# Head, tile slots and last tile of a fused linear-attention and feed-forward kernel moved

## The chip, the cores and the metric

The kernel runs on one core of one Trainium2 chip. The metric is the device time of one execution in microseconds; before the change the median of 12 executions is 298.38 us (297.88 to 298.96).

## The reference

Eight batches of 8 heads, 576 positions and 64 channels per head go through linear attention without softmax, an RMS norm per head, and a feed-forward block with a layer norm in front and a residual around it (model width 512, hidden width 2048):

```python
kv = np.einsum('bhsd,bhse->bhde', k, v)
out = np.einsum('bhsd,bhde->bhse', q, kv)
rms = np.sqrt(np.mean(out * out, axis=-1, keepdims=True) + 1e-06)
attn = out / rms * g_norm                 # then (b, h, s, d) -> x of shape (b, s, 512)

mu, var = mean and variance of x over the 512 channels
xn = (x - mu) / np.sqrt(var + 1e-06) * g_ln
y = x + np.maximum(xn @ w_ch1, 0.0) @ w_ch2
```

## The kernel before

**Tiles.** A batch has 576 positions: four main tiles of 128, and 64 left over. Two batches share one remainder tile, so every odd batch (1, 3, 5, 7) adds one. The order of the feed-forward work on TensorE is fixed: batch 0 to 7, then a block "rem" of the four remainder tiles. Each block is a first stage `mm1` (L391: x times w1, ScalarE evacuates with a ReLU, L404) and a second stage `mm2` (L438: times w2, 16 matmuls per tile, L417; VectorE adds the residual in `finish`, L422, and SyncE writes the tile out in two halves, L435 and L436).

**Slots.** Everything else (attention, norms, turns, loads) is hung between these matmuls. `at(slot, fn)` (L457) enters a function into an agenda, and `tick` (L460), called before every group of 16 matmuls or so (a PSUM bank of `mm1`, four matmuls of `mm2`), runs what stands under the slot's whole number, in order of the fraction. A block has 32 slots: 16 of the first stage, then 16 of the second; batch b starts at slot 32b. A slot sets only the place in each engine's instruction stream; each engine works its own stream in order, and waits on semaphores for the others. GpSimd's and SyncE's streams hold mainly DMA issues and so run far from the slot's time.

**A tile.** `o` (L254) multiplies q, turned, by the block-diagonal kv of two heads; `sq` squares it on ScalarE (L265), `red` sums on VectorE (L286), `root` takes the root on ScalarE (L296), then on VectorE `inv` (L303), `y` (L291), `x` (L310, with the sum for the mean) and `xc` (L320, mean removed and scaled by g_ln). `var` (L328, ScalarE) gives the variance, used only in `finish` as `rstd`. `turn` (L331) brings xc into the layout that `mm1` takes, in four 128x128 transposes on TensorE and a ScalarE copy (L336, L338), or with one DMA transpose from SyncE (L340). `plan_tile` (L359) puts o, sq and red at slot s, y, x and xc at s + 2, var at s + 6, and the turn at a slot given to it.

**q and kv.** `kv_of(b)` (L228) makes kv in 40 matmuls and two ScalarE copies. From batch 2 on, q is turned by `turn_q_dma` (L199): a VectorE copy into q_p (L201), then one DMA transpose from SyncE into qt (L203). `load_batch` (L96) issues six loads of k, v and q from GpSimd, behind a one-element copy from qt of the batch before (L98), so that they start when that turn has landed.

**PSUM.** Eight banks in four pools: `ps_m` ("misc", 1), `ps_out` ("ops", 2, products of tiles), `ps1` ("p1", 3, first stage), `ps2` ("p2", 2, second stage).

**The head.** Batch 0 has no earlier matmuls to hide behind. `fill` (L193) runs dummy matmuls while k and v load. `kv_first` (L207) makes kv of batch 0, and kv_g, the same scaled by g_norm. Tiles 0 and 1 are then done in halves of four heads: `half_o` (L485) turns the q of both tiles on TensorE with 64x64 transposes (`turn_groups`, L177), copies the turns to SBUF (ScalarE for the first half, VectorE for the second, L490), and multiplies by kv (L497). `half_sq` (L503) and `half_red` (L507) follow; `o_g` and `x_g` (L267, L274) take x from the product with kv_g, which saves the y step. The xc of tile 0 is made and turned in two column halves (L529 to L534). The q of tiles 2, 3 and of the remainder is turned later by `turn_first` (L188), in slots.

Of the kernel before, what the change touches and what calls it, by code (L numbers as in the profile page):

```python
# [14 lines left out]
def kernel(  # L15
# [11 lines left out]
    nc = tc.nc  # L27
# [160 lines left out]
    def turn_first(i, pool, tag):  # L188
        tp = pool.tile([128, HP, 128], bf16, tag=tag, name="tp")
        n = turn_groups(tp, i, 0, H)  # L190
        nc.scalar.copy(qts[0][:, i, :, :n], tp[:, :, :n])

    def fill(n):  # L193
        for _ in range(n):
            p1 = ps2.tile([128, 512], f32, tag="p2", name="p1")
            nc.tensor.matmul(p1, lhsT=fill_sb[:, :128], rhs=fill_sb, start=True, stop=True)  # L196
            del p1
# [145 lines left out]
    def main_tile(b, j, pool=None, tag="ops"):  # L343
        q_t, kvp = qts[b], held[b]
        if b not in blks:
            blks[b] = new_block("main", 3)
        return Tile([(slice(0, 128), lambda hp: q_t[:, j, hp, :], kvp)], blks[b], j, pool, tag)
# [90 lines left out]
    def mm2(b, split_last=False):  # L438
        for ts in range(4):
            if split_last and ts == 3:  # L440
                for c0 in (0, Dm // 2):
                    p2 = ps2.tile([128, Dm], f32, tag="p2", name="p2")
                    mm2_part(b, ts, p2, 0, nDe, c0, c0 + Dm // 2)
                    finish(b, ts, p2, c0, c0 + Dm // 2, both=True)
                    del p2
            else:
                p2 = ps2.tile([128, Dm], f32, tag="p2", name="p2")
                mm2_part(b, ts, p2, 0, nDe)
                finish(b, ts, p2)
                del p2  # L450
        del blks[b], m1s[b]
# [22 lines left out]
    fill(24)  # L474
# [3 lines left out]
    t = [main_tile(0, i) for i in range(4)]  # L478
# [6 lines left out]
    def half_o(half):  # L485
        hp0 = half * HP // 2
        tp = ps2.tile([128, 2, HP // 2, 128], bf16, tag="p2", name="tp")
        for i in range(2):
            turn_groups(tp[:, i], i, 2 * hp0, 2 * hp0 + H // 2)
            copies[half][i](qts[0][:, i, hp0:hp0 + HP // 2], tp[:, i])  # L490
        res = []
        for i in range(2):
            pool, tag = banks[half][i]
            o = pool.tile([128, H // 2, D], f32, tag=tag, name="o_half")
            flat = o.rearrange("p h e -> p (h e)")
            for k2 in range(HP // 2):
                nc.tensor.matmul(flat[:, k2 * 128:(k2 + 1) * 128], lhsT=qts[0][:, i, hp0 + k2, :],  # L497
                                 rhs=kv_pack[0][:, hp0 + k2, :], start=True, stop=True)
            res.append(o)
        return res  # L500

    def half_sq(i, half, o):
        nc.scalar.activation(sqs[i][:, half * H // 2:(half + 1) * H // 2], o, func=AF.Square)  # L503
# [4 lines left out]

    oa = half_o(0)
    half_sq(0, 0, oa[0])  # L510
    half_sq(1, 0, oa[1])
    ob = half_o(1)
    half_sq(0, 1, ob[0])
    half_sq(1, 1, ob[1])
    for half in range(2):
        half_red(0, half)
    half_red(1, 0)
    half_red(1, 1)
    del oa, ob, sqs
    t[0].o_g(ps1, "p1")  # L520
    t[1].o_g(ps1, "p1")
    fill(5)
    t[0].x_g()
    t[1].root()
    x_blk, st, xT = t[0].blk
    for i in range(2):
        cs = slice(i * Dm // 2, (i + 1) * Dm // 2)
        xc = work.tile([128, Dm // 2], bf16, tag="xch", bufs=2, name="xc")
        nc.vector.scalar_tensor_tensor(xc, in0=x_blk[:, 0, cs], scalar=st[:, 1, 0:1],  # L529
                                       in1=g_ln_sb[:, cs], op0=ALU.add, op1=ALU.mult)  # L530
        tp = ps_out.tile([128, 2, 128], bf16, tag="ops", name="tp")
        for kk in range(2):
            nc.tensor.transpose(tp[:, kk, :], xc[:, kk * 128:(kk + 1) * 128], identity)
        nc.scalar.copy(xT[:, 2 * i:2 * i + 2, :128], tp)  # L534
        del xc, tp
    t[1].x_g()
    t[1].xc()
# [24 lines left out]
    at(0, lambda: turn_first(2, ps_m, "misc"))  # L562
    at(2, lambda: t[1].turn(True))
    at(2.1, o2)
    at(2.2, x2)
    at(4, lambda: turn_first(3, ps_m, "misc"))
    at(5, lambda: t[3].o())
    at(5.5, x3)
# [3 lines left out]
    at(11, lambda: t[3].turn(True))  # L572
# [20 lines left out]
    for j, s, tn in ((0, 24, 29), (1, 27, 34), (2, 31, 38), (3, 35, 42)):  # L593
        plan_tile(s, lambda j=j: main_tile(1, j), tn, True)
# [9 lines left out]
    at(47, lambda: load_batch(3, qts[2][:1, J, HP - 1, 127:]))  # L604
    at(57, lambda: kv_of(3))
    at(57.5, lambda: turn_q_dma(3))
    for b in range(3, B):
        s = 32 * b
        if b > 3:
            at(s - 60, lambda b=b: load_batch(b, qts[b - 1][:1, J, HP - 1, 127:]))  # L610
            at(s - 39, lambda b=b: kv_of(b))
            at(s - 38, lambda b=b: turn_q_dma(b))
        for j in range(J):
            o = s - 28 + (0, 5, 10, 15)[j]
            plan_tile(o, lambda b=b, j=j: main_tile(b, j), o + 6, False)
        if b % 2:
            plan_tile(s - 11, lambda b=b: rem_tile(b), s - 5, False)
        at(s + 14, lambda b=b: rstd_of(b))
# [58 lines left out]
```

## Time and profile before

| | |
|---|---|
| Median of 12 executions | 298.38 us (297.88 to 298.96) |
| The execution that was profiled | 297.88 us |
| Its span, first to last instruction | 296.1 us |
| TensorE busy | 282.8 us (96%) |
| ScalarE, VectorE busy | 157.2 us, 149.7 us |
| Granted TensorE clock, mean | 0.998 |
| First matmul with w1 | 16.98 us from the span's start |
| End of the last matmul | 292.08 us |

A row of a timeline gives start, duration, engine, line, operation, what is written from what, shapes, and how often; in brackets stands the idle time ahead of it and what ended it. A wait row gives who waited for whom: total, times, longest. "L401 PE" is TensorE at line 401 of the kernel. Matmuls overlap, so a row's duration is longer than its share of the engine: a 128x512 matmul lasts 379 ns and the next starts 216 ns after it. Durations of copies and of VectorE operations overlap their successors by some 60 to 80 ns.

### The profile page before, as it was taken

The page shows a single profiled execution, that of the slowest core. Times are in us where ns is not written, and L with a number is a line of the kernel's source. Part 1 is how long each engine was busy: PE and PEld are TensorE (multiplying, and loading weights), DVE is VectorE, ACT ScalarE, POOL GpSimd, SP SyncE. Part 2 cuts the span into 40 slices and gives each one's busy share as a digit, 9 for nine tenths or more (in the row PEclk, how much of TensorE's full clock was granted, in tenths as well). Part 3 has the DMA queues.
Part 4 walks back from the last instruction along what each step waited for, and adds up shares of the span by engine and source line. Part 5 has one row for each costly group of instructions (what it writes and reads, how often), then busy time and mean ns, then how long its engine had stood idle before and what let it go on. Part 6 is the DMA issues. An engine that isn't in the chain of part 4 may idle for free.

```text
span 296.1 us, 5729 instructions
## 1 busy us (share of the span) xinstructions
PE 282.8 (96%) x2280; PEld 159.3 (54%) x2305; DVE 149.7 (51%) x332; ACT 157.2 (53%) x341; POOL 40.7 (14%) x68
## 2 busy tenths in 40 slices
PE   8879999999999999999999999999999899999994
PEld 3469854996579644445444544444444344444443
DVE  5657018836995794468246953692369500220022
ACT  3457754886559742774187517931793266016500
POOL 8433500032023000500050005000000000000000
PEclk9999999999999999999999999999999999999999
DMA  7999999469579926995799249967312330131033
GB/s 214 203 206 203 201 202 198 95 99 185 119 144 175 138 54 130 166 194 81 149 169 164 55 93 158 202 110 136 78 35 44 69 84 0 38 74 32 0 73 71
DMA packets 63130, 35.84 MB, mean 121 GB/s; under 512 B 30716, under 2 KB 58108, under 8 KB 63104
## 3 DMA queue, kind: packets, MB, share of 16 engines
q0 software_dynamic: 28016, 17.76, 42.3%
q1 hardware_dynamic: 34656, 16.99, 28.3%
q10 hardware_dynamic: 432, 0.72, 0.7%
q8 instruction: 18, 0.29, 0.4%
q14 instruction: 8, 0.07, 0.1%
HBM read 36.71 MB, written 9.44 MB: 156 GB/s over the span
## 4 chain that ended last, share of the span: by engine, by line
PE 74%; DVE 12%; ACT 4%; DMA 4%; issue 3%; SPq 1%; DVEq 0%
PE p L401 38%; PE p L417 28%; DMA qt<-q_p 3%; DVE x_blk L310 2%; PE p L196 2%; DVE y L291 2%; PE o_ps L259 2%; DVE o_sb L422 2%; ACT m L404 2%; DVE xc L320 1%; PE kv_ps L234 1%; DVE ss L286 1%; DMA xT_blk<-xc 1%; PE tp L183 1%; PE tp L336 1%
## 5 line engine op out<-in xcount | busy, mean ns | idle before, releaser
L401 PE MATMUL p<-xT_blk,w_sb 128*128 128x128 bf16 (+2 forms) x1015 | 131.2, 285 | 1.5 <-ACT xT_blk L338 0.7
L417 PE MATMUL p<-w_sb,m 128*128 128x512 bf16 (+1 forms) x576 | 128.6, 373 | 2.8 <-DVE o_sb L422 1.4
L404 ACT ACTIVATE m<-p 128x512 bf16<-128x512 f32 x144 | 85.7, 597 | 65.9 <-PE p L401 64.7
L401 PEld LDWEIGHTS <-w_sb 128*128 128x128 bf16 x1024 | 78.5, 98 | 46.5 <-issue 2.0
L417 PEld LDWEIGHTS <-m 128*128 128x128 bf16 x592 | 56.2, 98 | 62.0 <-issue 2.3
L422 DVE SCALAR_TENSOR_TENSOR o_sb<-p,rstd,x_blk 128x512 f32<-128x512 f32 (+1 forms) x37 | 27.0, 732 | 43.1 <-PE p L417 40.4
L286 DVE TENSOR_REDUCE ss<-sq 128x8 f32<-128x512 f32 x34 | 23.2, 683 | 26.5 <-ACT sq L265 26.5
L328 ACT ACTIVATE dev<-x_blk,st_blk 128x512 f32<-128x512 f32 x36 | 25.8, 716 | 7.2 <-DVE st_blk L314 7.2
L265 ACT ACTIVATE sq<-o_ps 128x512 f32<-128x512 f32 x34 | 20.2, 595 | 15.5 <-PE o_ps L259 15.2
L320 DVE SCALAR_TENSOR_TENSOR xc<-x_blk,st_blk,g_ln_sb 128x512 bf16<-128x512 f32 x35 | 26.3, 751 | 1.2
L291 DVE TENSOR_TENSOR y<-o_ps,inv 128x512 f32<-128x512 f32 x34 | 23.5, 692 | 2.7
L310 DVE SCALAR_TENSOR_TENSOR x_blk<-y,g_norm_sb 128x512 f32<-128x512 f32 x34 | 23.5, 692 | 1.2
L410 DVE RECIPROCAL rstd<-rstd 128x4 f32<-128x4 f32 x9 | 1.6, 174 | 39.8 <-ACT rstd L409 39.8
L296 ACT ACTIVATE rms<-ss,eps_sb 128x8 f32<-128x8 f32 x36 | 10.8, 301 | 14.0 <-DVE ss L286 13.6
L303 DVE RECIPROCAL inv<-rms 128x8 f32<-128x8 f32 x36 | 7.2, 199 | 21.4 <-ACT rms L296 21.3
L98 POOL COPY gate<-qt 1x1 bf16<-1x1 bf16 x5 | 0.9, 177 | 123.3 <-DMA qt<-q_p 123.3
L259 PEld LDWEIGHTS <-qt 128*128 128x128 bf16 (+1 forms) x152 | 9.9, 100 | 8.3 <-issue 1.7
L259 PE MATMUL o_ps<-kv_pack,qt 128*128 128x128 bf16 (+1 forms) x152 | 13.3, 220 | 0.7 <-DMA qt<-q_p 0.7
L196 PE MATMUL p<-fill_sb 128*128 128x512 bf16 x29 | 8.3, 450 | 1.2 <-DVE eps_sb L137 1.2
L338 ACT COPY xT_blk<-tp 128x512 bf16<-128x512 bf16 x11 | 6.4, 582 | 3.4 <-PE tp L336 3.4
L328 ACT ACTIVATION_READ_ACCUMULATOR dev<-x_blk,st_blk 128x1 f32 x36 | 6.9, 192 | 0.0
L234 PEld LDWEIGHTS <-k_in 128*64 128x64 bf16 x280 | 5.4, 112 | 2.6 <-issue 2.5
(78 smaller groups left out, 116.0 us busy)
## 6 DMA issues: line engine op xcount, KB each, us to landing
out_dram<-o_sb SPq DMA_DIRECT2D x70, 128.0 KB, 2.4
w_sb<-in_moe_w_ch_dram POOLq DMA_DIRECT2D x8, 512.0 KB, 14.0
k_in<-in_k_dram POOLq DMA_DIRECT2D x7, 320.0 KB, 5.5
v_in<-in_v_dram POOLq DMA_DIRECT2D x7, 320.0 KB, 8.1
q_in<-in_q_dram POOLq DMA_DIRECT2D x7, 320.0 KB, 10.3
q_in<-in_q_dram POOLq DMA_DIRECT2D x8, 256.0 KB, 11.0
k_in<-in_k_dram POOLq DMA_DIRECT2D x7, 256.0 KB, 6.5
v_in<-in_v_dram POOLq DMA_DIRECT2D x7, 256.0 KB, 8.8
```

What stands on the lines that cost most here:

```text
L196: nc.tensor.matmul(p1, lhsT=fill_sb[:, :128], rhs=fill_sb, start=True, stop=True)
L259: nc.tensor.matmul(flat[rows, hp * 128:(hp + 1) * 128], lhsT=lhsT_of(hp), rhs=kvp[:, hp, :], start=True, stop=True)
L265: nc.scalar.activation(self.sq_t, self.o_ps, func=AF.Square)
L286: nc.vector.tensor_reduce(self.ss, self.sq_t, axis=AX.X, op=ALU.add)
L291: nc.vector.tensor_mul(self.y_t, self.o_ps, self.inv().to_broadcast([128, H, D]))
L310: nc.vector.scalar_tensor_tensor(x_blk[:, ts].rearrange("p (h d) -> p h d", h=H), in0=self.y_t, scalar=1.0, in1=g_norm_sb.to_broadcast([12 ...
L320: nc.vector.scalar_tensor_tensor(self.xc_t, in0=x_blk[:, self.ts], scalar=st[:, 1, self.ts:self.ts + 1], in1=g_ln_sb, op0=ALU.add, op1=ALU ...
L328: nc.scalar.activation(dev, x_blk[:, ts], func=AF.Square, bias=st[:, 1, ts:ts + 1], accum_out=st[:, 2, ts:ts + 1])
L401: nc.tensor.matmul(p1[:, i, :], lhsT=w1_sb[:, kk, de * 128:(de + 1) * 128], rhs=blk[2][:, kk, sl], start=(kk == 0), stop=(kk == nK - 1))
L404: nc.scalar.activation(m1[:, de0:de0 + per, sl], p1, func=AF.Relu)
L417: nc.tensor.matmul(p2[:, c0:c1], lhsT=m1s[b][:, de, ts * 128:(ts + 1) * 128], rhs=w2_sb[:, de, c0:c1], start=(de == 0), stop=(de == nDe - 1))
L422: nc.vector.scalar_tensor_tensor(o_sb[:, c0:c1], in0=p2[:, c0:c1], scalar=rstds[b][:, ts:ts + 1], in1=blks[b][0][:, ts, c0:c1], op0=ALU.mu ...
```

## The change

- **Fills.** 18 in place of 24 at the start; two more after the first turns, in the pool of tile products; 8 in place of 5 ahead of tile 0's xc.
- **Tiles 0 and 1.** The turns of both tiles stand ahead of their copies, each in a PSUM tile of its own. The products come one by one, each with its square, between the turns of the second half. The root of tile 0 stands ahead of tile 1's reduces. The products of tiles 2 and 3 go to pool `ps2`.
- **Tile 1's x** is made and turned in two column halves, as tile 0's was.
- **Slots of batch 0.** The q turn of tile 2 moves from slot 0 to 1, and VectorE copies it; the turn of tile 1's xc, the product of tile 2 and its x move from slot 2 to slot 1. Tile 3's x stays in slot 5, its turn moves from 11 to 10.
- **Batch 1.** The turn of its first tile moves from slot 29 to 30.
- **Batches 3 to 7.** With s = 32b: the products move from s - 28, -23, -18, -13 to s - 31, -26, -21, -16 for batch 3 and to s - 33, -28, -23, -18 for the others, with all that `plan_tile` hangs on them. The remainder tile moves from s - 11 to s - 14. kv moves from s - 39 to s - 41 (batch 3) or s - 45, and the DMA turn of q, in whole slots, from s - 39 to s - 40 (batch 3) and from s - 38 to s - 44 (others). The places of the loads in the program stay.
- **Last tile.** Its second stage and output run in columns of 256, 128 and 128 in place of 256 and 256.

```diff
-    def turn_first(i, pool, tag):
+    def turn_first(i, pool, tag, copy=nc.scalar.copy):
...
-        nc.scalar.copy(qts[0][:, i, :, :n], tp[:, :, :n])
+        copy(qts[0][:, i, :, :n], tp[:, :, :n])
-    def fill(n):
+    def fill(n, pool=ps2, tag="p2"):
...
-                for c0 in (0, Dm // 2):
+                for c0, c1 in ((0, 256), (256, 384), (384, Dm)):
...
-    fill(24)
+    fill(18)
-    t = [main_tile(0, i) for i in range(4)]
+    t = [main_tile(0, i, ps2, "p2") for i in range(4)]
...
-    def half_o(half):
+    def half_turn(half):
         hp0 = half * HP // 2
-        tp = ps2.tile([128, 2, HP // 2, 128], bf16, tag="p2", name="tp")
+        tps = [ps2.tile([128, HP // 2, 128], bf16, tag="p2", name="tp") for _ in range(2)]
         for i in range(2):
-            turn_groups(tp[:, i], i, 2 * hp0, 2 * hp0 + H // 2)
-            copies[half][i](qts[0][:, i, hp0:hp0 + HP // 2], tp[:, i])
+            turn_groups(tps[i], i, 2 * hp0, 2 * hp0 + H // 2)
+        for i in range(2):
+            copies[half][i](qts[0][:, i, hp0:hp0 + HP // 2], tps[i])
+    def half_o(i, half):
+        (one tile's half product, and its square)
...
+    half_turn(0)
+    fill(2, ps_out, "ops")
+    half_o(0, 0)
+    half_turn(1)
+    half_o(1, 0)
+    half_o(0, 1)
+    half_red(0, 0)
+    half_red(0, 1)
+    half_o(1, 1)
+    t[0].root()
     half_red(1, 0)
     half_red(1, 1)
     t[0].o_g(ps1, "p1")
     t[1].o_g(ps1, "p1")
-    fill(5)
+    fill(8)
     t[0].x_g()
     t[1].root()
...
+    halves_turn(0, halves_xc(0), ps_out, "ops")
     t[1].x_g()
-    t[1].xc()
+    xc1 = list(halves_xc(1))
-    at(0, lambda: turn_first(2, ps_m, "misc"))
-    at(2, lambda: t[1].turn(True))
-    at(2.1, o2)
-    at(2.2, x2)
+    at(1, lambda: turn_first(2, ps_m, "misc", nc.vector.tensor_copy))
+    at(1.1, lambda: halves_turn(1, xc1, ps_out, "ops"))
+    at(1.2, o2)
+    at(1.3, x2)
...
-    at(5.5, x3)
+    at(5.1, x3)
-    at(11, lambda: t[3].turn(True))
+    at(10, lambda: t[3].turn(True))
-    for j, s, tn in ((0, 24, 29), (1, 27, 34), (2, 31, 38), (3, 35, 42)):
+    for j, s, tn in ((0, 24, 30), (1, 27, 34), (2, 31, 38), (3, 35, 42)):
...
     for b in range(3, B):
         s = 32 * b
+        at(47 if b == 3 else s - 60,
+           lambda b=b: load_batch(b, qts[b - 1][:1, J, HP - 1, 127:]))
+        d = -41 if b == 3 else -45
+        at(s + d, lambda b=b: kv_of(b))
+        at(s + d + 1.7, lambda b=b: turn_q_dma(b))
         for j in range(J):
-            o = s - 28 + (0, 5, 10, 15)[j]
+            o = s + d + (10 if b == 3 else 12) + 5 * j
             plan_tile(o, lambda b=b, j=j: main_tile(b, j), o + 6, False)
         if b % 2:
-            plan_tile(s - 11, lambda b=b: rem_tile(b), s - 5, False)
+            plan_tile(s - 14, lambda b=b: rem_tile(b), s - 8, False)
```

## The prediction

> **What bounds the kernel now.** I read the busy shares first, then TensorE's waits, then the timelines of the places where it waits longest.
>
> ```profile
> PE 282.8 (96%) x2280; PEld 159.3 (54%) x2305; DVE 149.7 (51%) x332; ACT 157.2 (53%) x341; POOL 40.7 (14%) x68
> ```
>
> TensorE is busy for 282.8 of 296.1 us and no other engine is beyond 53%, so the end moves only if TensorE's idle time or its own work changes. 4.0 us of the idle time is the tail after its last matmul (292.08), 1.2 the start. The rest stands in its waits (line, awaited work, total, times, longest):
>
> ```profile
> PE p L417 <- DVE o_sb L422: 1.4, 3, 1.1
> PE tp L533 <- DVE xc L529: 1.2, 1, 1.2
> ...
> PE p L401 <- ACT xT_blk L338: 0.7, 1, 0.7
> PE o_ps L259 <- DMA qt<-q_p: 0.7, 2, 0.4
> ...
> PE tp L183 <- ACT qt L490: 0.5, 1, 0.5
> PE tp L183 <- DVE qt L490: 0.4, 1, 0.4
> PE tp L336 <- DVE xc L320: 0.2, 1, 0.2
> ```
>
> Two groups: the head, where tile 0 goes through one chain (turn, copy, product, square, reduce, root, x, xc, turn) before the first w1 matmul at 16.98, and three kinds of stall in the steady part. The head, by engine:
>
> ```profile
> 10.11 0.37 ACT L490 COPY qt<-tp 128x256 bf16<-128x256 bf16 x1
> 10.89 0.37 ACT L490 COPY qt<-tp 128x256 bf16<-128x256 bf16 x1 [0.40 <-PE tp L183]
> 11.89 0.29 DVE L490 COPY qt<-tp 128x256 bf16<-128x256 bf16 x1 [1.15 <-PE tp L183]
> 12.59 0.29 DVE L490 COPY qt<-tp 128x256 bf16<-128x256 bf16 x1 [0.41 <-PE tp L183]
> 14.53 0.69 DVE L277 SCALAR_TENSOR_TENSOR x_blk<-og_ps,inv 128x512 f32<-128x512 f32 x1
> 16.32 0.77 ACT L534 COPY xT_blk<-tp 128x256 bf16<-128x256 bf16 x2 [1.67 <-PE tp L533]
> 20.13 1.95 PE L401 MATMUL p<-xT_blk,w_sb 128*128 128x128 bf16 x32 [0.71 <-ACT xT_blk L338]
> ```
>
> Four q copies take turns with four turns, because the two tiles of a half share one PSUM tile; the last copy starts 2.5 us after the first. The last row is tile 1's first w1 matmul. The steady part:
>
> ```profile
> 180.16 0.40 PE L259 MATMUL o_ps<-kv_pack,qt 128*128 128x128 bf16 x4 [0.41 <-DMA qt<-q_p]
> ...
> 232.94 3.61 PE L417 MATMUL p<-w_sb,m 128*128 128x512 bf16 x16 [1.10 <-DVE o_sb L422]
> ```
>
> ```profile
> 231.48 0.75 DVE L320 SCALAR_TENSOR_TENSOR xc<-x_blk,st_blk,g_ln_sb 128x512 bf16<-128x512 f32 x1
> 232.14 1.41 DVE L422 SCALAR_TENSOR_TENSOR o_sb<-p,rstd,x_blk 128x512 f32<-128x512 f32 x2
> ```
>
> The second group shows why: VectorE evacuates the second output tile of batch 6 only at 232.14, since the chains of three tiles of batch 7 stand before it in its queue, and TensorE's fourth output tile waits for that PSUM buffer.
>
> **The change, part by part.** Times are of the profiled execution.
>
> *Fewer fills (24 to 18): 0.* Fills run 216 ns each (five in 1.24 us at 13.50), so they end near 7.0, not 8.3. But the first half of v lands at 7.47 and the second at 8.95, and the second half of the kv matmuls starts at 8.99 now. Only the first half moves forward; kv still ends at 9.75. Against it stands a rule of the Trainium skill (TensorE: Matmul & The Clock Gate, "The HAM clock gate" and Part 4): TensorE falls to half clock after an idle window of about 3.4 us, and turns don't count as busy. The trace: from the fills' end at 8.3 to the next fill at 13.50 there are 5.2 us of small matmuls, turns and gaps, and the stretch 8.2 to 17.0 has a granted clock of 1.00. The new stretch without fills is 7.0 to about 10.2, shorter, then two fills and later eight. By the rule as written this could cost up to 1.7 us (3.4 us at half speed); by the trace nothing. I take nothing.
>
> *Both turns ahead of the copies: -0.9.* From 9.75, with durations of the rows (a turn of 8 groups 0.2 to issue, its copy 0.37 on ScalarE or 0.29 on VectorE, half product 0.28, square 0.39, reduce 0.42 at a pitch of 0.33): copies at 10.11 and 10.45 on ScalarE; the two fills until 10.6; product of tile 0 at 10.62; second-half turns at 10.75 and 10.95 (their q landed at 10.52); VectorE copies at 11.11 and 11.37; products at 11.2, 11.45, 11.7; squares at 10.94, 11.50, 11.89, 12.29; reduces at 11.63, 12.37, 12.70, 13.03; root at 12.83; inverse at 13.36; x at 13.67 in place of 14.53. From here the chain is as before: first half of xT copied at 15.8 (16.69 before).
>
> *The w1 start: another -0.05.* Slot 0 now holds only matmuls (until 17.05, the second half of xT being late). Slot 1: third q turn 0.45, tile 1's x in halves 0.22 (its xc ends at 17.47), then the product of tile 2, which needs VectorE's copy of the 128x512 turn. No row has that shape. The 256-column row is 0.29; doubling gives 0.58. The skill (VectorE: DVE Perf Modes, "The perf-mode tier table") lets a bf16 copy out of PSUM run at twice the rate, which makes the further 256 columns about 0.13, so 0.42; the 64x128 f32 cast of 0.28 beside the 0.29 bf16 copy of twice the columns agrees with two rates. I take 0.45: the copy ends at 18.05, TensorE waits 0.4 behind it (0.55 with 0.58), slot 1's matmuls start at 18.3 (their w1 landed at 17.84) and tile 1's at 19.25 in place of 20.13: -0.9 in all. The old wait of 0.7 is traded for a new one of 0.4. If w1's second chunk is late by more than 0.5 us, the rest of the lead is lost with it.
>
> *Slots 2 to 15: +0.1, -0.2.* Three evacuations now stand before the copy of tile 3's q, which ends at about 22.6, where its product could start at 22.5: +0.1. Tile 3's turn in slot 10 lets its xT be ready; the present 0.2 us before slot 12 (30.72) goes.
>
> *Batch 1, first turn in slot 30: -0.25,* the whole wait on xc at 48.76 (xc ends 48.96, slot 30 starts at 49.4). The copy then ends by 51.5; it is needed at 52.0.
>
> *Batches 3 to 7, tiles three to five slots earlier: -1.45.* The three output waits are 0.16 (111.9), 0.18 (172.3) and 1.10. For batch 7, from the start of batch 6's second stage: xc of tile 3 ends at 3.75, reduce 4.4, first output 5.1, remainder chain (about 3.0) 8.2, second output 8.95; its buffer is needed at 12 slots of 0.863 plus 0.36, 10.7. No wait is left, with 1.75 to spare. With the q copy (0.82) between, batch 6's is ready at 10.05, needed at 11.7.
>
> *The q turn by DMA and kv six slots earlier: 0.* The waits on qt are 0.24 (119.4) and 0.41. The turn moves with its reader: now 10 slots apart, then 11. But the q copy comes behind the remainder chain on VectorE, and SyncE issues it after an output and, for batch 6, a transpose of tile 3. Batch 6: chain 8.55, copy 9.3, issue 9.45, landed 5.05 later (175.04 to 180.16 shows 5.1) at 14.5; the product stands at 15 slots plus kv 1.0 plus 0.36: 14.3. Wait 0.2. Batch 4: landed 15.0, wanted 14.55; wait 0.5. Batches 5 and 7 have no remainder tile in the way: landed 13.1, wanted 13.95. So 0.65 goes and about 0.65 comes; ends -0.65 and +0.6. The loads behind each turn start earlier by as much: for batch 4 v lands at about 96 and kv wants it at 104, so no cost on GpSimd's queue. Batch 3's copy stands at 77.97 in VectorE's order and its q lands at 76.93: hidden, with 1.0 to spare.
>
> *Batch 3's first tile at slot 65: +0.3.* ScalarE's root for it waits for a reduce that VectorE reaches only after the remainder chain (xc until 88.93), so until 89.6; the evacuations behind it slip, and slot 71, at 91.86, finds its buffer free at about 92.25. Ends 0 and 0.5.
>
> *Last tile in 256, 128, 128: -0.1.* The final output op falls from 0.48 to about 0.35 (0.75 for 512 columns gives 1.03 ns each); narrow matmuls add some 0.04.
>
> Sum: -0.9 + 0.1 - 0.2 - 0.25 - 1.45 + 0 + 0.3 - 0.1 = -2.5, rounded to -2.4 for waits too small to list. The execution profiled took 297.88, its span 296.1 and 1.8 around it; I expect 293.7 and 295.5. The median shown is 0.5 above that execution: 298.38 - 2.4 = **296.0 us**.
>
> **Rivals.** *The head's lead is half lost* to w1's second chunk or to the 0.58 copy and ScalarE's crowded slots 1 to 5: for it, the margin of 0.5; against it, the landings don't depend on TensorE. 296.6.
>
> *The output stall moves rather than goes:* VectorE has as much work as before, 14.25 of 16.5 us busy between 68.5 and 85. If the 1.1 comes back elsewhere: 297.2, partly within what can be told from nothing.
>
> *Slower:* each product of batches 4 to 7 waits for its q turn in the last slot of a second stage, one for one. The lead is used up when the four waits sum to 2.4 + 0.65, 0.75 each; that is from a landing 0.25 to 1.6 later than I worked out. At 0.97 each it is 4 x 0.97 - 0.65 - 2.4 = +0.8: 299.2. For it: VectorE and SyncE are both in order and the copy is now behind a whole chain; a transpose among loads took 8.4 us (88.96 to 97.37). Against it: the loads of the batch before have landed by then.
>
> *The change does nothing in the steady part,* because the DMA landings and not the slots set the order: against it, two of the three output waits have VectorE alone in front.
>
> **How the numbers follow.** As forecast 0.55 (295.4 to 296.5); half the head 0.14; stall moved 0.20, of which 0.05 lands within 0.2%; slower 0.11. A measurement of this kernel tells about 0.2% (0.6 us) from no change. So faster 0.84, same 0.05, slower 0.11. The range, 295.1 to 298.0, takes in the first three and leaves the slower case out.
>
> **What the profile after would show.** First w1 matmul near 15.9, tile 1's near 19.3; a new wait of 0.4 of the product on VectorE's copy; none on o_sb; waits on qt of 0.2 to 0.5 at batches 4 and 6; a small one near slot 71; an end of the last matmul near 289.8. The forecast is wrong if waits on qt exceed 1 us in sum, or if the granted clock drops before 17 us.

## The result, and the profile after

The kernel after takes 293.43 us in the median of 8 runs (292.96 to 294.21), the kernel before 298.36 (32 runs, 297.79 to 299.06): a ratio of 0.9835, 95% interval 0.9825 to 0.9845. That is 4.9 us faster; the prediction was 2.4 (296.0, range 295.1 to 298.0). The sign and most of the places were right, the size was half of what came. The profiled executions are 297.88 us before and 292.96 after, their spans 296.1 and 291.2, so the pair of traces shows the same 4.9 us.

The page's busy shares after:

```profile
PE 282.2 (97%) x2294; PEld 159.6 (55%) x2320; DVE 150.8 (52%) x335; ACT 154.8 (53%) x341; POOL 41.0 (14%) x68
```

TensorE's busy time is 0.6 us less; the rest of the gain is idle time. TensorE's waits after, all that the view lists (who waited for whom: total, times, longest):

```profile
PE p L196 <- DVE eps_sb L137: 1.2, 1, 1.2
PE tp L540 <- DVE xc L531: 0.8, 1, 0.8
PE p L417 <- issue: 0.8, 5, 0.2
PE even L219 <- DMA v_in<-in_v_dram: 0.2, 1, 0.2
PE p L401 <- ACT m L404: 0.2, 1, 0.2
PE o_ps L259 <- DVE qt L191: 0.2, 1, 0.2
PE p L196 <- issue: 0.2, 1, 0.2
PE p L417 <- PE kv_ps L234: 0.2, 1, 0.2
```

The output waits (L417 on o_sb), the waits on qt by DMA and the wait on xc before slot 30 have left the list. New are slot 71 (L401 on ScalarE's m), the product of tile 2 behind VectorE's copy (L259), and 0.2 for the second half of v (L219). The head, in the timelines of ScalarE, VectorE and TensorE:

```profile
10.11 0.65 ACT L491 COPY qt<-tp 128x256 bf16<-128x256 bf16 x2
11.13 0.49 DVE L491 COPY qt<-tp 128x256 bf16<-128x256 bf16 x2 [0.49 <-PE tp L183]
13.51 0.69 DVE L277 SCALAR_TENSOR_TENSOR x_blk<-og_ps,inv 128x512 f32<-128x512 f32 x1
15.72 1.34 PE L401 MATMUL p<-xT_blk,w_sb 128*128 128x128 bf16 x16
17.48 0.42 DVE L191 COPY qt<-tp 128x512 bf16<-128x512 bf16 x1
17.96 0.40 PE L259 MATMUL o_ps<-kv_pack,qt 128*128 128x128 bf16 x4 [0.20 <-DVE qt L191]
18.19 2.84 PE L401 MATMUL p<-xT_blk,w_sb 128*128 128x128 bf16 x48
```

The two copies of a half now run back to back (x2 in one row), the last ends at 11.62 instead of 12.88, x starts at 13.51 (14.53 before), the first w1 matmul at 15.72 (16.98). The end of batch 6's second stage, where 1.10 stood before, on VectorE and on TensorE:

```profile
225.69 0.75 DVE L422 SCALAR_TENSOR_TENSOR o_sb<-p,rstd,x_blk 128x512 f32<-128x512 f32 x1
228.88 0.75 DVE L422 SCALAR_TENSOR_TENSOR o_sb<-p,rstd,x_blk 128x512 f32<-128x512 f32 x1 [2.44 <-PE p L417]
232.34 0.75 DVE L422 SCALAR_TENSOR_TENSOR o_sb<-p,rstd,x_blk 128x512 f32<-128x512 f32 x1 [2.70 <-PE p L417]
225.66 6.64 PE L417 MATMUL p<-w_sb,m 128*128 128x512 bf16 x29
```

VectorE now waits for TensorE (the brackets), not the other way round, and TensorE's w2 matmuls run without a gap. The start of each stage, read from the first matmul of L401 or L417, shows where the time came from (us):

| point | before | after | gained so far | gained in between |
|---|---|---|---|---|
| first w1 matmul | 16.98 | 15.72 | 1.26 | 1.26 |
| batch 1, first stage | 52.05 | 50.38 | 1.67 | 0.41 |
| batch 2, first stage | 84.93 | 83.23 | 1.70 | 0.03 |
| batch 3, first stage | 115.82 | 114.36 | 1.46 | -0.24 |
| batch 4, first stage | 145.66 | 143.84 | 1.82 | 0.36 |
| batch 5, first stage | 176.14 | 173.73 | 2.41 | 0.59 |
| batch 6, first stage | 206.15 | 203.38 | 2.77 | 0.36 |
| batch 7, first stage | 236.62 | 232.13 | 4.49 | 1.72 |
| last matmul ends | 292.08 | 287.63 | 4.45 | -0.04 |
| span ends | 296.07 | 291.19 | 4.88 | 0.43 |

Batch 2 shows no gain and then a loss of 0.24: slot 71 lies there, and its second stage now also holds the first product of batch 4 (a product is 0.22, and one that has moved from a first stage into the second stage ahead of it shifts the boundaries by that much, without changing the end).

### The profile page after: what moved, and what is told of

Read it like the earlier page. It is cut to its first block, busy times and chain, and to the rows that moved or that the text cites. A ratio compares the mean times of both kernels' runs of the same rounds, so it can differ in the third digit from the quotient of the medians.

```text
span 291.2 us, 5775 instructions
## 1 busy us (share of the span) xinstructions
PE 282.2 (97%) x2294; PEld 159.6 (55%) x2320; DVE 150.8 (52%) x335; ACT 154.8 (53%) x341; POOL 41.0 (14%) x68
## 4 chain that ended last, share of the span: by engine, by line
PE 83%; DMA 6%; DVE 6%; ACT 2%; issue 2%; POOL 1%; SPq 0%; DVEq 0%; POOLq 0%
PE p L401 40%; PE p L417 36%; PE o_ps L259 2%; DMA q_in<-in_q_dram 2%; DMA out_dram<-o_sb 2%; DMA qt<-q_p 2%; PE kv_ps L234 2%; DVE o_sb L422 1%; DVE ss L286 1%; ACT m L404 1%; DVE x_blk L310 1%; DVE y L291 1%; PE tp L183 1%; DVE xc L320 1%; PE p L196 1%
## 5 line engine op out<-in xcount | busy, mean ns | idle before, releaser
L401 PE MATMUL p<-xT_blk,w_sb 128*128 128x128 bf16 (+2 forms) x1018 | 131.7, 285 | 0.8 <-ACT m L404 0.2
L417 PE MATMUL p<-w_sb,m 128*128 128x512 bf16 (+2 forms) x589 | 126.9, 368 | 1.6 <-issue 0.8
L401 PEld LDWEIGHTS <-w_sb 128*128 128x128 bf16 x1024 | 78.7, 98 | 45.4 <-issue 1.0
L417 PEld LDWEIGHTS <-m 128*128 128x128 bf16 x608 | 56.5, 98 | 60.4
L422 DVE SCALAR_TENSOR_TENSOR o_sb<-p,rstd,x_blk 128x512 f32<-128x512 f32 (+2 forms) x38 | 27.3, 719 | 44.5 <-PE p L417 41.8
L320 DVE SCALAR_TENSOR_TENSOR xc<-x_blk,st_blk,g_ln_sb 128x512 bf16<-128x512 f32 x34 | 25.6, 752 | 1.2
L98 POOL COPY gate<-qt 1x1 bf16<-1x1 bf16 x5 | 0.9, 177 | 115.4 <-DMA qt<-q_p 115.4
L259 PEld LDWEIGHTS <-qt 128*128 128x128 bf16 (+1 forms) x152 | 9.7, 100 | 8.1 <-DMA qt<-q_p 1.7
L259 PE MATMUL o_ps<-kv_pack,qt 128*128 128x128 bf16 (+1 forms) x152 | 13.3, 221 | 0.3 <-DVE qt L191 0.2
L196 PE MATMUL p<-fill_sb 128*128 128x512 bf16 x27 | 9.1, 502 | 1.4 <-DVE eps_sb L137 1.2
L338 ACT COPY xT_blk<-tp 128x512 bf16<-128x512 bf16 x10 | 5.8, 579 | 2.3 <-PE tp L336 2.3
L237 ACT CAST kv_pack<-kv_ps 64x256 bf16<-64x256 f32 x7 | 2.6, 366 | 8.1 <-PE kv_ps L234 8.0
## 6 DMA issues: line engine op xcount, KB each, us to landing
q_in<-in_q_dram POOLq DMA_DIRECT2D x8, 256.0 KB, 12.7
```

The lines of the kernel that those rows point to most:

```text
L259: nc.tensor.matmul(flat[rows, hp * 128:(hp + 1) * 128], lhsT=lhsT_of(hp), rhs=kvp[:, hp, :], start=True, stop=True)
L320: nc.vector.scalar_tensor_tensor(self.xc_t, in0=x_blk[:, self.ts], scalar=st[:, 1, self.ts:self.ts + 1], in1=g_ln_sb, op0=ALU.add, op1=ALU ...
L401: nc.tensor.matmul(p1[:, i, :], lhsT=w1_sb[:, kk, de * 128:(de + 1) * 128], rhs=blk[2][:, kk, sl], start=(kk == 0), stop=(kk == nK - 1))
L417: nc.tensor.matmul(p2[:, c0:c1], lhsT=m1s[b][:, de, ts * 128:(ts + 1) * 128], rhs=w2_sb[:, de, c0:c1], start=(de == 0), stop=(de == nDe - 1))
L422: nc.vector.scalar_tensor_tensor(o_sb[:, c0:c1], in0=p2[:, c0:c1], scalar=rstds[b][:, ts:ts + 1], in1=blks[b][0][:, ts, c0:c1], op0=ALU.mu ...
```

## Experiments

Two theories of the size. **S (sizes):** the steps of the prediction are right, but a wait was costed by its idle time, which begins at the modelled end of the matmul before it. A 128x512 matmul lasts 0.379 us and the next normally starts 0.216 after it, so a wait shown as w delays the start by w + 0.163, and a delay below 0.163 shows no wait at all. The longest output wait of before as an example:

```profile
225.63 6.22 PE L417 MATMUL p<-w_sb,m 128*128 128x512 bf16 x27
```

Its last matmul ends at about 231.84 and so started at 231.46; the next one starts at 232.94, 1.48 later. Less the usual 0.216 that is a delay of 1.26, where the list shows 1.10. From start to start the output waits of before are 0.33 + 0.35 + 1.26 = 1.94 (shown 1.45), those on qt 0.40 + 0.57 = 0.97 (0.65), slot 30's 0.41 (0.25), and three first stages start 0.29, 0.24 and 0.22 late for an xT (shown as 0.13, 0.08 and 0.06, not counted in the forecast). **P:** the sizes of the forecast hold and something else gave the rest. The rivals within it are the tail, the head and the clock.

**The last tile alone.** [e1_tail]

```diff
-                for c0 in (0, Dm // 2):
+                for c0, c1 in ((0, 256), (256, 384), (384, Dm)):
...
```

> The kernel before with the last tile alone in columns of 256, 128, 128. The prediction's sum (a shorter last VectorE operation only): -0.1 us. The trace after, where the time from the last matmul to the end is 3.56 in place of 3.99: -0.4 us, because the last write is also smaller and lands sooner.

297.82 us, ratio 0.998 (0.9968 to 0.9992). Of 12 executions the four with a full clock (below) took 297.39 to 297.53, 0.4 under 297.86, the median of the kernel before at full clock. So the tail is worth 0.4, not 0.1. In its trace the time from the last matmul to the end is 3.55 (3.99 before). VectorE's last operation before, and then the end of the kernel after:

```profile
292.12 0.48 DVE L422 SCALAR_TENSOR_TENSOR o_sb<-p,rstd,x_blk 128x256 f32<-128x256 f32 x1 [1.26 <-PE p L417]
...
286.39 2.12 SPq L435 DMA_DIRECT2D out_dram<-o_sb  x3
286.77 0.35 DVE L422 SCALAR_TENSOR_TENSOR o_sb<-p,rstd,x_blk 128x128 f32<-128x128 f32 x1 [0.41 <-PE p L417]
287.67 0.35 DVE L422 SCALAR_TENSOR_TENSOR o_sb<-p,rstd,x_blk 128x128 f32<-128x128 f32 x1 [0.54 <-PE p L417]
```

The operation is 0.13 shorter, as forecast. The last write behind it lands 2.05 us after its issue instead of 2.22 (it is half as large), and the time from that landing to the end of the span is 1.09 instead of 1.21. The last two, 0.29 together, were not in the sum.

**The head alone** [e2_head] (fills, turns ahead of copies, slots of batch 0; batch 1's turn, batches 3 to 7 and the last tile as before; the diff is that part of the change).

> The kernel before with batch 0's part of the change alone (fills, turns ahead of copies, halves of tile 1, slots 0 to 10). The prediction's sum: -0.9 + 0.1 - 0.2 = -1.0 us. By the trace after, where the second stage of batch 0 starts 1.25 earlier: -1.25 us. Rival, a lead that is given back later to transfers: under -0.8 us.

296.55 us, ratio 0.9946 (0.9933 to 0.9959), the five runs within 296.52 to 296.62. All five had full clock; against 297.86 that is 1.3: the head gives the 1.25 that the two traces show up to batch 0's second stage, with no sign of a lead lost later.

**Batch 1's first turn in slot 30 alone.** [e3_turn30]

```diff
-    for j, s, tn in ((0, 24, 29), (1, 27, 34), (2, 31, 38), (3, 35, 42)):
+    for j, s, tn in ((0, 24, 30), (1, 27, 34), (2, 31, 38), (3, 35, 42)):
```

> The kernel before with only the turn of batch 1's first tile moved from slot 29 to 30. Theory A, a wait costs the idle time that the waits show (0.25): -0.25 us. Theory B, it costs the delay from one matmul's start to the next beyond the usual 0.216, since the idle time is counted only from the end of a matmul that lasts 0.38: -0.41 us.

297.9 us, ratio 0.9981 (0.9971 to 0.9992); the five full-clock executions 297.35 to 297.60, median 0.47 under 297.86. Nearer to 0.41 than to 0.25. Its trace leaves the head out of the comparison: from the first w1 matmul to batch 1's first stage it takes 34.65 where before takes 35.07, 0.42 less. One wait, one gain, and its size is that of S.

**Batches 3 to 7 alone.** [e4_steady]

```diff
...
-            at(s - 39, lambda b=b: kv_of(b))
-            at(s - 38, lambda b=b: turn_q_dma(b))
+        d = -41 if b == 3 else -45
+        at(s + d, lambda b=b: kv_of(b))
+        at(s + d + 1.7, lambda b=b: turn_q_dma(b))
...
-            o = s - 28 + (0, 5, 10, 15)[j]
+            o = s + d + (10 if b == 3 else 12) + 5 * j
-            plan_tile(s - 11, lambda b=b: rem_tile(b), s - 5, False)
+            plan_tile(s - 14, lambda b=b: rem_tile(b), s - 8, False)
```

> The kernel before with batches 3 to 7 moved alone (products, remainder tiles, kv, DMA turns). Prediction: -1.45 for the output waits, 0 for the turns, +0.3 at slot 71: -1.15 us. Theory B with the trace after: output waits 1.26 + 0.33 + 0.35 = 1.94, turns of q 0.97 less 0.41, starts of first stages that wait for a DMA turn of x 0.75, less 0.38 at slot 71: -2.9 us.

295.6 us, ratio 0.9914 (0.9902 to 0.9926), which is 2.6 us; its one full-clock execution is 2.8 under 297.86 (295.06). Its trace tells it more sharply, since the head can be left out: from the first w1 matmul (17.56) to the end of the last matmul (289.76) it takes 272.20, before 275.10, so 2.90. S stands: 1.94 + 0.75 + 0.97 less what is left on qt (0.36 in its trace) less slot 71 (0.38) is 2.92. The forecast's own terms gave 1.15.

In the traces the four parts sum to 0.44 + 1.33 + 0.42 + 2.90 = 5.1, beside the 4.88 between the spans: they add up within 0.2. The medians at full clock add up less well: 0.4 + 1.3 + 0.5 + 2.8 = 5.0, but from 297.86 to the 293.43 of the kernel after it is 4.4. The profiled execution of the kernel after lies 0.47 under that kernel's own median; of this, only 0.2 is traced (the last run below), and the rest is open.

**Which move carries it: without the remainder tile's** [o3_remstays] (e4_steady with the remainder left at s - 11).

```diff
-            plan_tile(s - 14, lambda b=b: rem_tile(b), s - 8, False)
+            plan_tile(s - 11, lambda b=b: rem_tile(b), s - 5, False)
```

> The kernel before with batches 3 to 7 moved as in the change, but the remainder tiles left at s - 11. Theory P, the output waits come from the remainder chain standing late: they return, 1 us or more lost against the run that moved both (295.6). Theory Q, they come from three tiles' chains within one second stage, and with the main tiles five slots earlier VectorE keeps up wherever the remainder stands: no wait on o_sb, within 0.3 us of 295.6.

295.38 us, ratio 0.9909 (0.9894 to 0.9924), the same as e4_steady. The main tiles' earlier slots remove the output waits; the remainder's move adds nothing that can be measured.

**And with the turn alone:** [o4_turnonly] kv and the q turn of batches 4 to 7 earlier, all tiles left.

```diff
-            at(s - 39, lambda b=b: kv_of(b))
-            at(s - 38, lambda b=b: turn_q_dma(b))
+            at(s - 45, lambda b=b: kv_of(b))
+            at(s - 44, lambda b=b: turn_q_dma(b))
```

> The kernel before with only kv and the DMA turn of q of batches 4 to 7 moved to s - 45 and s - 44, the tiles left. By delay from matmul start to start, the two waits on qt go (0.40 + 0.57) and the q copies leave the places ahead of the output operations of the second stages, the output wait of 1.26 stays: -0.9 to -1.2 us. By idle time as the prediction counted, -0.65 us. Rival, the turn gets behind the remainder chain and lands as late: 0.

310.97 us, ratio 1.0436 (1.0412 to 1.0461): 12.7 slower, where 0.65 to 1.2 faster was expected. Its waits on TensorE, and then SyncE's and GpSimd's timelines at batch 4's turn:

```profile
PE p L401 <- DMA xT_blk<-xc: 10.2, 3, 6.0
PE p L417 <- DVE o_sb L422: 3.3, 3, 1.1
```

```profile
108.45 3.04 SPq L203 DMA_TRANSPOSE qt<-q_p  x1
...
114.66 2.71 SPq L340 DMA_TRANSPOSE xT_blk<-xc  x2
...
114.37 0.18 POOL L98 COPY gate<-qt 1x1 bf16<-1x1 bf16 x1 [22.45 <-DMA qt<-q_p]
114.88 0.68 POOL L93 DMA_DIRECT2D k_in<-in_k_dram  x1 [0.33 <-issue]
```

The q turn lands at 114.25, and the one-element copy at L98 lets batch 5's six loads go at 114.88. The two xc transposes of the tiles, left where they were, are issued at 114.66 and 116.01 and so run among the loads: they land 5.7 and 9.2 us later. Before, the turn lands at 119.63, the transposes are issued at 113.20 and 117.72 and land 2.5 us later each, and the loads start at 120.26. TensorE waits, start to start, 3.5, 6.2, 1.0 and 0.2 for an xT: 10.9 against 0.75. The output waits are 3.77 against 1.94, because the q copy now stands ahead of a tile's chain on VectorE. The qt waits (0.97) are gone. That is 10.2 + 1.8 - 1.0 = 11.0 of the 13.1 us between the spans. In the rest lie a head that is 0.53 later than in the trace of before (see the clock, below) and a window of TensorE at half clock behind the longest wait (columns: stretch, its length, busy time of TensorE, its weight loads, VectorE, ScalarE and GpSimd with their instructions, granted clock, DMA share, GB/s):

```profile
181.00:187.20 6.20, 0.48 (x3) 0.10 (x1) 0.75 (x1) 0.00 (x0) 1.41 (x3) 0.97 1.43 173
187.20:190.20 3.00, 2.70 (x7) 1.01 (x7) 0.00 (x0) 0.60 (x1) 0.00 (x0) 0.50 1.27 236
```

**Loads or order?** Two runs leave out the loads of batches 5 to 7 (these are worked out from old data), in the kernel before [p1_before_noload] and in that of o4_turnonly [p2_turn_noload]:

```diff
-            at(s - 60, lambda b=b: load_batch(b, qts[b - 1][:1, J, HP - 1, 127:]))
+            if b == 4:
+                at(s - 60, lambda b=b: load_batch(b, qts[b - 1][:1, J, HP - 1, 127:]))
```

> The kernel before without the loads of k, v and q for batches 5 to 7 (these batches are worked out from what lies in the buffers, so their outputs are not the reference's; all else is the same work). It is the yardstick of the next run. Both theories: the waits of first-stage starts on a transposed xc (0.29, 0.24, 0.22 us from start to start) are the only ones that the loads can cause here, so 298.3 less 0 to 0.75: 297.5 to 298.3.

298.62 us, ratio 1.0011 (0.9998 to 1.0024): no gain. The xT waits of before (0.27 and 0.22 at batches 3 and 5 in this trace) stay without the loads, so these loads are not their cause.

> The kernel of the run o4_turnonly (kv and the q turn by DMA of batches 4 to 7 earlier, tiles left), again without the loads of batches 5 to 7. Theory L (loads): there the turn's earlier landing lets the next batch's loads start before two tile transposes, which then take 6 to 9 us among them in place of 2.5; without the loads the waits on xT (10.9 us) go, the output waits stay (3.8 against 1.9) and the qt waits (1.0) are gone, so about 1 us above p1_before_noload: 298.0 to 299.5. Theory O (order): the tile transposes are late because the q copy on VectorE and the q turn on SyncE now stand in front of them; then leaving out the loads saves little, and the time stays above 306.

300.66 us, ratio 1.0089 (1.0073 to 1.0104):

```profile
PE p L417 <- DVE o_sb L422: 3.3, 3, 1.1
...
PE p L401 <- DMA xT_blk<-xc: 1.0, 2, 0.9
```

10.3 of the 12.7 are gone with the loads. The 2.0 above p1_before_noload are the part that theory O meant: the same 3.3 on o_sb, and four xT delays of 1.8 from start to start. Theory L was right about the main part, its number 1.2 too low. In the change the tiles move with the turn, so that this price is not paid (a transpose issued at 113.95 there lands 6.9 us later and nothing waits for it): the forecast's "no cost" for the earlier loads holds only because of that, and the forecast had not said so.

**The fills.** [o2_fill24]

```diff
-    fill(18)
+    fill(24)
```

> The changed kernel with 24 fills at the start in place of 18. The prediction's step: v lands at 8.9, so the fills' number is worth nothing: no change in the head's times. Rival, the earlier first half of kv is worth its 0.7 us or part of it: 0.3 to 0.7 us slower.

The kernel after with 24 fills takes 293.33 us (four runs, 292.69 to 293.48), ratio 0.983 (0.9812 to 0.9849): no difference in the medians. Its trace has one: the fills end at 9.11 instead of 8.03, kv at 10.36 instead of 9.70, and the first w1 matmul starts at 16.32, 0.60 later than in the kernel after. 0.35 of it is left at the end of the span, since the first product of batch 7 does not wait for its qt in this execution (0.20 in the kernel after). So the fills' number is not always free; the clock, below, shows when.

**The copy of tile 2's q,** [o1_scalarcopy] on ScalarE in the kernel after:

```diff
-    at(1, lambda: turn_first(2, ps_m, "misc", nc.vector.tensor_copy))
+    at(1, lambda: turn_first(2, ps_m, "misc"))
```

> The changed kernel with the copy of tile 2's q turn on ScalarE, as before, in slot 1. It stands there behind an evacuation that ends at 17.69 and ahead of tile 1's two xT copies, and takes 0.59 in place of VectorE's 0.42: the product of tile 2 waits until about 18.35 rather than 17.96, so +0.4 us. Rival, the copy is hidden either way: no change.

293.4 us, ratio 0.9839 (0.9824 to 0.9854), the median of the kernel after. Its trace shows the expected wait, but smaller:

```profile
17.64 0.58 ACT L191 COPY qt<-tp 128x512 bf16<-128x512 bf16 x1
18.28 0.40 PE L259 MATMUL o_ps<-kv_pack,qt 128*128 128x128 bf16 x4 [0.46 <-ACT qt L191]
```

The product comes 0.27 later after its turn than behind VectorE's copy, and its span is 0.3 longer (291.5); the medians, with a spread of 1 us among executions of the kernel after, can't tell that. The expected 0.4 was too much; in this pair of traces the choice of engine is worth 0.3.

**The clock.** The kernel before has two kinds of executions. Of 64 beside the experiments, 20 have a mean granted clock of 0.997 or more and take 297.67 to 298.12 (median 297.86); 44 have 0.994 or less and take 298.11 to 299.44 (median 298.6). Traces of the second kind show one window of 3.41 us at half clock in the head. The stretches of e4_steady, whose head is that of before (columns as above):

```profile
9.50:12.97 3.47, 2.17 (x84) 1.64 (x76) 1.93 (x7) 1.93 (x6) 1.93 (x3) 1.00 1.28 203
12.97:16.38 3.41, 3.35 (x22) 1.78 (x17) 3.09 (x10) 1.37 (x4) 1.23 (x2) 0.50 1.31 206
```

and the same head in the execution of before that the prediction read:

```profile
9.50:13.00 3.50, 2.23 (x55) 1.41 (x49) 1.83 (x7) 1.87 (x6) 1.91 (x3) 1.00 1.29 206
13.00:16.40 3.40, 2.04 (x18) 1.02 (x18) 3.22 (x11) 1.26 (x5) 1.23 (x2) 1.00 1.31 203
```

But most of the 0.7 is not the price of this window. The two kinds also differ in their fills. In every trace the first fills start 0.43 us apart and the later ones 0.22; the change comes between 3.9 and 7.2 us, in before at 4.8, in e4_steady at 6.1, in the kernel after at 6.8 (the granted clock is given as 1.00 all through). All fills of these three, in this order:

```profile
1.20 7.09 PE L196 MATMUL p<-fill_sb 128*128 128x512 bf16 x24 [1.20 <-DVE eps_sb L137]
1.20 7.78 PE L196 MATMUL p<-fill_sb 128*128 128x512 bf16 x24 [1.20 <-DVE eps_sb L137]
1.20 6.83 PE L196 MATMUL p<-fill_sb 128*128 128x512 bf16 x18 [1.20 <-DVE eps_sb L137]
```

| traces with the head of before | fills end | kv ends | first w1 matmul | between these two |
|---|---|---|---|---|
| full clock, or half clock only after 17.8 (before, p2_turn_noload, e1_tail) | 7.9 to 8.3 | 9.6 to 9.8 | 16.9 to 17.0 | 7.23 to 7.29 |
| half clock between 12.7 and 17.2 (e3_turn30, e4_steady, o3_remstays, o4_turnonly, p1_before_noload) | 8.9 to 9.4 | 10.1 to 10.6 | 17.5 to 17.8 | 7.23 to 7.40 |

The last column is the stretch in which the window lies, and it is longer by 0.2 at most. What makes the second kind late by 0.5 to 0.9 is that its 24 fills run slowly for longer, end after v has landed (8.95), and hold up kv. A window that falls later costs more: in e1_tail it begins at 17.8, where the w1 matmuls run, and the first w2 matmul comes 18.63 after the first w1 matmul, before 17.58. With 18 fills, in seven traces (after, e2_head, n1_nofill2, n3_turn46, n4_b3, o1_scalarcopy, p3_after_again), kv ends at 9.6 to 9.9 wherever the change lies.

All eleven executions of the kernel after had a mean granted clock of 0.997 or more. To see what does that, the two fills between the turns were taken out of the kernel after [n1_nofill2], and two were put into the kernel before [n2_before_fill2]:

```diff
-    fill(2, ps_out, "ops")
```

> The changed kernel without the two fills after the first turns (those eight ahead of tile 0's xc stay). Theory C, TensorE's clock halves for 3.4 us in executions whose head has some 5 us without dense matmuls, and the two fills prevent it: mean granted clock 0.994 in more than half of the executions, and a median 0.5 us above the changed kernel's, 293.9 or more. Rival, the shorter chain of the head or the eight fills hold the clock: 0.997 or more throughout, and the same time or 0.1 less.

293.77 us, ratio 0.9851 (0.9834 to 0.9868); two of four executions had the half-clock window (293.98 and 294.14 against 293.49 and 293.56). In its trace the window begins at 11.3, and the first w1 matmul comes 0.45 later than in the kernel after, though kv ends at the same time.

```diff
...
+    fill(2, ps1, "p1")
     ob = half_o(1)
```

> The kernel before with two fills added between the first half's products and the second half's turns, nothing else. Theory C: granted clock 0.997 or more in every execution, and a median of about 298.0 to 298.3 with a small spread (the half clock gone, up to 0.4 us of TensorE's time added to the chain). Rival, the added fills only lengthen the chain: 0.994 as often as before, 298.9.

298.6 us, ratio 1.0009 (0.9998 to 1.0021). The window appears in 3 of 12 executions only, but the full-clock ones take 298.15 to 298.88: there the fills stand ahead of the second turns and, by this time, lengthen the chain by about as much as the clock gives. With the fills the window is rarer, as far as so few executions tell; it is not excluded: the next run, with the fills, shows it too.

**What is left in the kernel after.** The DMA turn of q at s - 46, one slot ahead of its kv [n3_turn46]:

```diff
-        at(s + d + 1.7, lambda b=b: turn_q_dma(b))
+        at(s + d + 1.7 if b == 3 else s - 46, lambda b=b: turn_q_dma(b))
```

> The changed kernel with the DMA turn of q of batches 4 to 7 two slots earlier (slot s - 46), ahead of the remainder tile's chain on VectorE. Theory, the two remaining waits on qt (0.21 and 0.20 in the trace, more in executions with later landings) go and nothing else waits: -0.4 us, a smaller spread between executions. Rival, VectorE's output operations slip by 0.8 and stall TensorE: no gain or up to 0.5 slower.

293.21 us, ratio 0.983 (0.9808 to 0.9853). No wait on qt is left in its trace; two of four executions fell to the half clock in the head (293.8), the other two took 292.49 and 292.60. Then, besides, batch 3's products at s - 29, -25, -20, -16 [n4_b3]:

```diff
-            o = s + d + (10 if b == 3 else 12) + 5 * j
+            o = s + ((-29, -25, -20, -16)[j] if b == 3 else -33 + 5 * j)
```

> As the one before, and batch 3's products at slots s - 29, -25, -20, -16. Theory, the stall of 0.38 at slot 71 comes from ScalarE's root waiting for VectorE behind the remainder chain of batch 1, and two slots later it is gone: another -0.4 us, about 292.6 in all. Rival, the crowding only moves to a later slot: no change.

**292.06 us** (292.03 to 292.41), ratio 0.9795 (0.9779 to 0.9811), 1.4 under the kernel after; by the ratio 6.1 under the kernel before that it ran beside. Its waits on TensorE, complete:

```profile
PE even L219 <- DMA v_in<-in_v_dram: 1.6, 2, 0.9
PE p L196 <- DVE eps_sb L137: 1.2, 1, 1.2
PE tp L540 <- DVE xc L531: 0.8, 1, 0.8
PE o_ps L259 <- DVE qt L191: 0.2, 1, 0.2
```

Slot 71 and the qt waits are gone, and all that remains stands in the first 18 us.

**The kernel after once more,** [p3_after_again] for a second trace.

> The kernel after, unchanged, for a second trace of it: the profiled execution (292.96) is 0.5 below its median (293.43) at the same granted clock. Theory W: what differs between executions is the waits on qt of batches 4 to 7 (0.21 and 0.20 in the first trace), so an execution at 293.4 or above shows 0.3 to 1.0 us more of them. Rival: it lies ahead of the first w1 matmul (landings of the first loads) or in the tail.

293.15 us (two runs), ratio 0.9837 (0.9817 to 0.9856). The second trace's span is 0.2 longer than the first, and the traces agree to 0.03 us until the end of batch 3's second stage, where the first product of batch 5 waits 0.20 for its qt (at 142.9), beside those of batches 4 and 7. So 0.2 of the spread lies in the qt waits; that executions at 294 differ by them too was not seen.

## Why the prediction was right and wrong

Its sum against the two traces, step by step, delays taken from start to start:

| step | forecast | traces |
|---|---|---|
| fewer fills | 0 | 0 in this pair (0.6 in the trace of o2_fill24) |
| head, until tile 1's w1 | -0.9 | -1.03 (20.13 to 19.10) |
| slots 2 to 15 | +0.1 - 0.2 | -0.22 |
| batch 1, slot 30 | -0.25 | -0.42 |
| output waits | -1.45 | -1.94 |
| q turn, qt waits | 0 | -0.56 (0.97 to 0.41) |
| first stages that wait for xT | not listed | -0.75 |
| slot 71 | +0.3 | +0.38 |
| tail | -0.1 | -0.43 |
| sum | -2.5 | -4.97 (span: -4.88) |

**Right:** the order of the parts, and the waits with their places, but for one on qt. x was 0.16 earlier than worked out, the first w1 matmul at 15.72 (near 15.9), tile 1's at 19.10 (near 19.3), the new wait of tile 2's product 0.36 from start to start (0.4), the output waits gone, slot 71 at 0.38. The copy of 512 columns took 0.42 us, the value worked out from two rates (the Trainium skill, VectorE: DVE Perf Modes, "The perf-mode tier table"); the doubled row's 0.58 would have been wrong.

**Wrong, the step "Batches 3 to 7":** "The three output waits are 0.16, 0.18 and 1.10" took the idle column for the delay: 1.45 was forecast, 1.94 came. The text before the prediction has the two numbers that correct it (0.379 and 0.216). For the three output waits, the two on qt and slot 30 this is six times 0.163, 1.0 us. The same step left out three first stages that start late for an xT, because the list shows next to nothing for them: 0.75 us. The sum even took 0.1 off "for waits too small to list", while these went away. e3_turn30 shows the size for one wait and e4_steady for all (2.90 by its trace, 1.15 by the forecast's terms). The end of the last matmul, forecast near 289.8, came at 287.63, and 293.43 lies below every case that the prediction weighed.

**Wrong, the step "The q turn by DMA":** "0.65 goes and about 0.65 comes". It was 0.97 that went and 0.41 that came. Counted from the start of the second stage in which it stands, batch 4's turn landed at 14.27 (forecast 15.0), and the product waited 0.21 (0.5). Batch 6's q copy ended at 9.24 (9.3), its turn landed at 14.25 (14.5), and nothing waited (0.2). But batch 7, for which 13.1 and no wait were forecast, landed at 14.02, and its product waited 0.20; its turn took 6.1 us from issue to landing, where 5.05 was reckoned. So the total came out lower because of batches 4 and 6, and one of the two waits that are left stands at a batch for which none was forecast.

**Wrong, the tail:** only the shorter VectorE operation was counted, not the smaller last write and its end (0.29).

**Wrong for a reason that the pair of traces does not show, the fills and the clock:** "Fewer fills: 0" and "by the trace nothing" read one execution, one of the third that keep full clock in the kernel before. In it the fills quickened at 4.8 us and ended before v landed. In the trace of the kernel after they quickened only at 6.8, and the 18 fills ended at 8.03, not near 7.0; the 0 held all the same, because v landed at 8.94. Most executions behind the median of before are of the other kind (of six such traces with this head, all have a half-clock window and five have late fills). That median is 0.5 above the full-clock one (298.36 to 297.86), and the kernel after has no such execution. Most of this 0.5 is likely owed to having six fills fewer, by the table above, and a part to the two added ones, by n1_nofill2 and n2_before_fill2. It is not shown: o2_fill24 has the same median as the kernel after, and the kernel before was not run with 18 fills and nothing else changed. In the medians it is made up for by another 0.5, by which the kernel after's profiled execution is below its own median at the same clock. So the 4.9 of the medians and the 4.9 of the traces agree by two halves of different kinds, which is chance.

The rule weighed there (the Trainium skill, TensorE: Matmul & The Clock Gate, "The HAM clock gate") was held against the change, with an estimate of 1.7 us from its 3.4 us; the window cost 0.2 at most where it fell ahead of the first w1 matmul in the head before, about 0.5 in n1_nofill2, and 1.0 behind that matmul in e1_tail. The same section says that the window runs freely, whatever the kernel does, and that where it falls varies from run to run. The runs fit that: in the nine traces with a half-clock window in the head it begins 6.8 us after the fills quicken (seven traces), or 10.2 or 13.7 (n3_turn46, e1_tail), which is two, three and four times its length of 3.41. By this, one trace can't show the clock of a head.

**The rivals:** the head was not half lost; no output wait came back elsewhere; the qt waits came to 0.41 and not to 3. What the slower rival feared, a transpose among loads, is real and large, but for the tiles' xT rather than for q, and only when the turn moves without the tiles (o4_turnonly).

## What to carry to other kernels

Cost a wait of TensorE from start to start: shown idle time plus the difference between a matmul's duration and its pitch, here 0.16 us each, and look for delayed starts that no wait row lists; over six waits this was 1.0 us here. A transfer whose landing opens the next loads should be moved together with the transposes that those loads would otherwise meet (12.7 us in o4_turnonly). A trace of a head is one execution: look at the granted clock of all runs, and at when the first matmuls quicken, before saying that fills or a clock window cost nothing.

## What was not expected of the hardware

- The first fills start 0.43 us apart, later ones 0.22; in 17 traces the change comes anywhere from 3.9 to 7.2 us. So 24 fills end anywhere from 7.9 to 9.4, and 18 from 6.6 to 8.2.
- In two thirds of its executions (44 of 64) the kernel before has a mean granted clock of 0.994 or less and is 0.7 us longer in the median. Where a trace shows it, the clock is 0.5 for one window of 3.41 us in the head, between 12.7 and 21.2 us. After a stall of 6.0 us in the steady part it fell too (o4_turnonly, at 187).
- A DMA transpose of one tile lands 2.5 us after its issue when no loads run (before, at 113.20 and 117.72), and 5.7 and 9.2 us after it among six loads (o4_turnonly, at 114.66 and 116.01).
- The last write lands 2.05 us after its issue with 128 columns, 2.22 with 256, and the span ends 1.09 and 1.21 after that: with half the bytes both together are 0.29 us shorter.
